# A fused attention and expert kernel: the last pair's half products in another order, one slot later, and the block sums queued ahead of the scalings

## The chip, the cores and the metric

The kernel runs on one core of a Trainium2 chip. The metric is the time of one execution on the device in microseconds; three runs of the kernel before gave 1199.53, 1202.34 and 1204.16 us (median 1202.34). The engines are named as the profile names them: PE is TensorE, which multiplies matrices (PEld is its loading of weights), DVE is VectorE, ACT is ScalarE, POOL is GpSimd and SP is SyncE, which here only issues DMA transfers. Each engine works through its own instructions in the order in which they stand.

## What is computed

There are two stages. The first is an attention without softmax, for 8 batches of 3008 rows; the second is a two-layer network on the 24064 rows that come out.

```python
scores = (1 / S) * z @ z.T                # z: (8, 3008, 64)
attn = maximum(scores, 0) ** 2
x = u * (attn @ v)                        # u, v: (8, 3008, 256)
h = x @ w_in                              # w_in: (256, 2048)
g = h / (1 + exp(-1.702 * h))
out = g @ w_out                           # w_out: (2048, 256)
```

Inputs and output are float32; the kernel multiplies in float16 and accumulates in float32.

## The kernel before, in words

A batch's 3008 rows are cut into six blocks of up to 512. `attend` computes the attention of one block as a list of small steps. The network of a batch follows in 48 calls of `up_group`, which I call slots 0 to 47. One slot makes a 512 x 256 piece of g (a tile `fg` of 256 of the 2048 hidden columns, for one block): four matmuls into `hg` (line 422), gelu by ACT into `gf` (line 435), and a scaling of `gf` into the float16 tile `gt`, by DVE (line 439) or, in slots 17 and up where the slot number modulo 8 is 1, 3 or 5, by ACT (line 437). `hg` shares two PSUM buffers with the score tiles `sc`, and `gf` has two buffers, so the matmuls of slot q wait for the gelu of slot q - 2, and the gelu of slot q for the scaling of slot q - 2.

Slots 0 to 15 are spread over the attention steps of block 4, the others follow the attention of block 5. For all but the end of the last batch, two blocks form a pair (blocks 0 and 1, 2 and 3, 4 and 5), so a pair takes 16 slots: eight tiles, each for both blocks. `TILES` sets the order of the tiles: 0, 4, 1, 5, 2, 6, 3, 7. In even batches block 5 takes part with 384 rows of a pair, and the rest of block 4 is a separate small product (`odd_block`); in odd batches both blocks have 512.

The second layer multiplies a pair as a 2 x 2 arrangement. With a11, a21 the low tiles of the pair's two blocks and a12, a22 the high ones, seven products (P1 to P7) take the place of eight. Four sums of tiles feed them, made by DVE in `pair_sum` for each of four tile pairs m = 0 to 3: S1 = a21 + a22 (line 547), S2 = S1 - a11 (line 549), S3 = a11 - a21 (line 542, written over a21) and S4 = a12 - S2 (line 551). `up_group` appends S1, S2 and S3 of tile pair m to the list `SUMS` in the slot that completes a22, and S4 one slot later; each slot draws one sum from the front of the list, two when it holds over eight.

`pair_product` issues half a product, four of its eight matmuls: the first half with m = 0 and 1, the second with m = 2 and 3 (line 585). P1, P5 and P2 each open a PSUM bank. P6, P7 and P4 go on adding into P1's bank, P3 into P5's. After each product the bank is read: copied into `y` by ACT for P1, P5, P6 and P4 (line 598), or added into `y` by DVE for P3, P7 and P2 (line 600). The next product on a bank can only start when that read has ended.

`products` lists the half products of a batch, and each slot from 16 on takes one from the list behind its `hg` matmuls: slots 16 to 43 run pairs 0 and 1, slots 44 to 47 the first four of the last pair. What is left runs as a tail after slot 47 (10 halves, 11 with the odd block), each step followed by sums still in `SUMS`. `store` turns a finished block on DVE (line 685, into the single buffer `yo`) and writes it by four DMAs from SP; the second block of a pair is stored two slots after its P4. In slots 30 and 36 DVE also turns a block of u for the next batch (line 202). From slot 44 on SP issues transposes for the next batch (line 298), one a slot and one a step of the tail.

The last batch has only two pairs; its blocks 4 and 5 go through `product`, one block at a time with fixed lists of names.

Of the kernel before, what the change touches and what calls it, by code (L numbers as in the profile page):

```python
# [15 lines left out]
def kernel(  # L16
# [24 lines left out]
    NCH = (S + CH - 1) // CH  # L41
# [5 lines left out]
    NFG = NFF // FFG  # L47
# [349 lines left out]
    def blocks(b):  # L397

        return [(i, CH if i < NCH - 1 or b % 2 else LFULL) for i in range(NCH)]

    def paired(b, s):

        return b < B - 1 or s < NCH // 2 - 1

    TILES = (0, 4, 1, 5, 2, 6, 3, 7)

    def up_group(b, q):
        s, r = divmod(q, 2 * NFG)
        pair = paired(b, s)
        if pair:  # L410
            fg, e = TILES[r // 2], r % 2
            if fg >= NFG // 2:
                e = 1 - e
            k = 2 * s + e
        else:
            k, fg = divmod(q, NFG)
        i, n = blocks(b)[k]
        hg = ps2.tile([P, FFG, CH], F32, name="hg", tag="ps2")
        for e in range(FFG):
            ff = fg * FFG + e  # L420
            for c in range(NCC):
                pe.matmul(  # L422
                    hg[:, e, :n], W1[:, c, ff * P:(ff + 1) * P], XT[b, i][:, c, :n],
                    start=(c == 0), stop=(c == NCC - 1),
                )
        if pair:
            if r % 2 == 0:
                GT[b, s, fg, "pair"] = pa.tile([P, FFG, 2, CH], F16, name="gt", tag="tt", bufs=14)
            g = GT[b, s, fg, "pair"][:, :, k % 2, :n]
        else:  # L430
            if fg % 2 == 0:
                GT[b, k, fg // 2] = pa.tile([P, CB, CH], F16, name="gt", tag="tt", bufs=14)
            g = GT[b, k, fg // 2][:, (fg % 2) * FFG:(fg % 2 + 1) * FFG, :n]
        gf = pw.tile([P, FFG, CH], F32, name="gf", tag="gf")
        act.activation(gf[:, :, :n], hg[:, :, :n], AF.Gelu_apprx_sigmoid, scale=1.0 / FSC)  # L435
        if q >= LAGY and q % 8 in (1, 3, 5):
            act.activation(g, gf[:, :, :n], AF.Copy, scale=FSC)  # L437
        else:
            dve.tensor_scalar(g, gf[:, :, :n], FSC, None, ALU.mult)  # L439
        for s_ in [SUMS.pop(0) for _ in range(min(len(SUMS), 1 + (len(SUMS) > 8)))]:  # L440
            s_()
        if pair:
            some = {2: ("S1", "S2", "S3"), 3: ("S4",)}.get(r % 4, ())
            SUMS.extend([lambda m=m, fg=fg: pair_sum(b, s, fg - NFG // 2, m) for m in some])
        elif fg in (NFG - 3, NFG - 1):
            SUMS.extend(left_sums(b, k, fg == NFG - 1))

# [2 lines left out]

    def pairs(b, k):
        return blocks(b)[k][1] // (2 * P)

    SUMS, ST = [], {}
# [32 lines left out]
    def left_sums(b, k, last):  # L490

        some = [("S1", 0), ("S2", 0)]
        if last:
            some = [("S1", 1), ("S2", 1)] + [(name, h) for name in ("S3", "S4") for h in range(2)]
        return [lambda m=m: left_sum(b, k, *m) for m in some]
# [16 lines left out]
    def products(b):  # L512

        lst = []
        for s in range(NCH // 2):
            if not paired(b, s):
                continue
            if s < NCH // 2 - 1:
                order = ["P1", "P1", "P5", "P5", "P6", "P6", "P3", "P3", "P7", "P7", "P2", "P2", "P4", "P4"]
            else:  # L520
                order = ["P1", "P1", "P5", "P2", "P5", "P2", "P6", "P6", "P3", "P3", "P7", "P7", "P4", "P4"]
                if blocks(b)[2 * s + 1][1] < CH:
                    order[6:6] = ["odd"]
            lst += [lambda s=s, m=m, h=order[:x].count(m): pair_product(b, s, m, h) for x, m in enumerate(order)]
        if not paired(b, NCH // 2 - 1):
            k = NCH - 2
            names = [(k, m) for m in ("P1", "P6", "P5", "P7", "P2")] + [(k + 1, "P1"), (k, "P4"), (k, "P3")]
            names += [(k + 1, m) for m in ("P6", "P5", "P7", "P2", "P4", "P3")]
            lst += [lambda k=k, m=m: product(b, k, m) for k, m in names]
        return lst  # L530

    def pair_part(b, s, name):

        f, e = {"a11": (0, 0), "a12": (1, 0), "a21": (0, 1), "a22": (1, 1)}[name]
        w = blocks(b)[2 * s + 1][1]
        return lambda m: GT[b, s, f * NFG // 2 + m, "pair"][:, :, e, :w]

    def pair_sum(b, s, m, name):
        a11, a12, a21, a22 = (pair_part(b, s, x)(m) for x in ("a11", "a12", "a21", "a22"))
        if name == "S3":  # L540
            ST[b, s, name, m] = a21
            dve.tensor_tensor(a21, a11, a21, ALU.subtract)  # L542
            return
        s_ = pa.tile([P, FFG, CH], F16, name="s", tag="a", bufs=26)
        s_ = ST[b, s, name, m] = s_[:, :, :blocks(b)[2 * s + 1][1]]
        if name == "S1":
            dve.tensor_tensor(s_, a21, a22, ALU.add)  # L547
        elif name == "S2":
            dve.tensor_tensor(s_, ST[b, s, "S1", m], a11, ALU.subtract)
        else:  # L550
            dve.tensor_tensor(s_, a12, ST[b, s, "S2", m], ALU.subtract)
# [229 lines left out]
    for b in range(B):  # L781
# [5 lines left out]
        for i in range(NCH):  # L787
# [4 lines left out]
            for n, step in enumerate(attend(b, i, b == 0 and i == 0)):  # L792
                if b == 0 and i == 0 and n in (5, 24):
                    load_u(0, n // 24)
                if b == 0 and i == 0 and n == 2:
                    copies = first_zt(3)
                if b == 0 and i == 0 and n == 3:
                    copies()
                if b == 0 and i == 0 and n in FIRST_CAST:
                    first_cast(FIRST_CAST[n], True)  # L800
                if b == 0 and i == 0 and n in FIRST_ZT:
                    first_zt(FIRST_ZT[n])()
                if (i, n) in turn:
                    turn_u(b, turn[i, n])
                if (i, n) in ((3, 3), (3, 26) if more else (4, 14)) and LAST2:
                    LAST2.pop(0)()
                if (i, n) in load:
                    load_u(b, load[i, n])
                if b == 0 and (i, n) in CASTW:
                    cast_w(CASTW[i, n])  # L810
                if b == 0 and (i, n) in LOADW:
                    load_w(LOADW[i, n])
                if more and (i, n) == (NCH - 2, 2 if b else 16):
                    load_z(b + 1)
                if b == 0 and i == NCH - 1 and n in (8, 30, 42):
                    wsums.pop(0)()
                take(host, sched[i].get(n, 0))
                if i == full(b) and n >= HEAD and (n - HEAD) * LAGY // (2 * NJ - 10) >= head and head < LAGY:
                    up_group(b, head)
                    head += 1  # L820
                step()
        late.sort(key=lambda t: t[0])
        if more:
            for i in range(2):
                load_u(b + 1, i)
            for n0 in range(0, NJ, VB):
                load_v(b + 1, n0)
        prods = products(b)
        for q in range(head, nup):
            if more and q in (head + 14, head + 20):  # L830
                k = int(q == head + 20)
                turn_u(b + 1, k)
                load_u(b + 1, k + 2)
            up_group(b, q)
            if b == 0 and q == head + 3:
                wsums.pop(0)()
            prods.pop(0)()
            for a_ in AFTER:
                a_[0] -= 1
            while AFTER and AFTER[0][0] < 0:  # L840
                AFTER.pop(0)[1]()
            if q >= 44 and late:
                late.pop(0)[1]()
# [42 lines left out]
```

## Time and profile before

| What | Value |
|---|---|
| median of three runs | 1202.34 us (1199.53 to 1204.16) |
| the profiled execution's own time | 1202.51 us |
| its span, first to last instruction | 1200.7 us |
| PE busy | 1171.5 us, 7996 matmuls |
| DVE busy | 862.8 us, 1386 instructions |
| ACT busy | 838.1 us, 941 instructions |
| POOL busy | 214.4 us |
| matmuls of `hg` (line 422) | 354.6 us busy, 1408 |
| gelu on ACT (line 435) | 1003 ns each, 384 |
| scaling on DVE (line 439) | 703 ns each, 288 |
| scaling on ACT (line 437) | 1022 ns each, 96 |
| copies of a bank by ACT (line 598) | 565 ns each, 92 |
| adds of a bank by DVE (line 600) | 665 ns each, 69 |

The span holds eight batches, which look alike in the trace; one is about 148 us long (the tail's matmuls that wait for the sum S1, for instance, lie at 304.51, 451.53 and 600.02 us). [...] A row of the timeline gives the start, the duration, the engine, the line, the operation, what it writes and reads with its shapes, the number of instructions merged, and in brackets the idle time before it with what ended it.

### The profile page before, as it was taken

The page shows a single profiled execution, that of the slowest core. Times are in us where ns is not written, and L with a number is a line of the kernel's source. Part 1 is how long each engine was busy: PE and PEld are TensorE (multiplying, and loading weights), DVE is VectorE, ACT ScalarE, POOL GpSimd, SP SyncE. Part 2 cuts the span into 40 slices and gives each one's busy share as a digit, 9 for nine tenths or more (in the row PEclk, how much of TensorE's full clock was granted, in tenths as well). Part 3 has the DMA queues.
Part 4 walks back from the last instruction along what each step waited for, and adds up shares of the span by engine and source line. Part 5 has one row for each costly group of instructions (what it writes and reads, how often), then busy time and mean ns, then how long its engine had stood idle before and what let it go on. Part 6 is the DMA issues. An engine that isn't in the chain of part 4 may idle for free.

```text
span 1200.7 us, 20853 instructions
## 1 busy us (share of the span) xinstructions
PE 1171.5 (98%) x7996; PEld 576.7 (48%) x7996; DVE 862.8 (72%) x1386; ACT 838.1 (70%) x941; POOL 214.4 (18%) x294
## 2 busy tenths in 40 slices
PE   9999999999999999999999999999999999899998
PEld 3544455444454445544445444554445544455446
DVE  7788866878668775587855877559776597664776
ACT  7878864688646886478864787647876578672785
POOL 3033201231012320133101331014200141101000
PEclk9999999999999999999999999999999999999999
DMA  9999498864898559966499865996559975696023
GB/s 222 210 115 125 86 160 154 96 92 97 152 152 103 89 101 171 147 93 95 95 160 146 103 94 105 167 150 91 92 102 161 141 105 89 108 174 131 1 36 71
DMA packets 459027, 143.47 MB, mean 119 GB/s; under 512 B 424624, under 2 KB 453040, under 8 KB 458928
## 3 DMA queue, kind: packets, MB, share of 16 engines
q1 hardware_dynamic: 402464, 102.36, 52.1%
q0 software_dynamic: 55104, 38.49, 22.0%
q8 instruction: 62, 1.02, 0.4%
q10 hardware_dynamic: 1360, 1.31, 0.3%
q14 instruction: 37, 0.30, 0.1%
HBM read 60.29 MB, written 24.64 MB: 71 GB/s over the span
## 4 chain that ended last, share of the span: by engine, by line
PE 91%; ACT 3%; issue 2%; DVE 2%; DMA 1%; ACTq 0%; POOL 0%; POOLq 0%
PE o L367 38%; PE hg L422 26%; PE st L585 21%; PE sc L235 5%; ACT gf L435 2%; DMA wst<-in_moe_w_in_dram 1%; PE st L631 1%; DVE gt L439 1%; PE yp L559 1%; ACT y L598 0%; DVE y L600 0%; ACT rl L256 0%; DVE s L547 0%; PE w L99 0%; DVE a L270 0%
## 5 line engine op out<-in xcount | busy, mean ns | idle before, releaser
L435 ACT ACTIVATE gf<-hg 128x1024 f32<-128x1024 f32 (+1 forms) x384 | 382.2, 1003 | 124.4 <-PE hg L422 114.2
L256 ACT ACTIVATE rl<-sc 128x1024 f16<-128x1024 f32 (+1 forms) x301 | 287.2, 993 | 141.7 <-PE sc L235 94.7
L422 PE MATMUL hg<-xt,W 128*128 128x512 f16 (+1 forms) x1408 | 354.6, 374 | 1.1 <-ACT gf L435 1.1
L367 PEld LDWEIGHTS <-V 64*128 64x128 f16 (+1 forms) x4098 | 240.4, 94 | 230.6 <-issue 9.3
L367 PE MATMUL o<-a,V 64*128 64x512 f16 (+3 forms) x2278 | 298.2, 368 | 0.3 <-DVE a L270 0.3
L439 DVE TENSOR_SCALAR gt<-gf 128x1024 f16<-128x1024 f32 (+1 forms) x288 | 202.6, 703 | 124.9 <-ACT gf L435 124.5
L270 DVE TENSOR_TENSOR a<-rl 128x1024 f16<-128x1024 f16 (+1 forms) x266 | 178.3, 674 | 126.4 <-ACT rl L256 123.2
L195 POOL DMA_DIRECT2D uq<-in_u_dram x168 | 115.5, 695 | 749.0 <-PE sc L235 550.6
L422 PEld LDWEIGHTS <-W 128*128 128x128 f16 x1536 | 149.6, 98 | 177.2 <-issue 4.2
L367 PE MATMUL o<-tt,V 64*128 64x512 f16 (+1 forms) x1518 | 234.0, 377 | 0.0
L235 PE MATMUL sc<-ZT 64*128 64x512 f16 (+3 forms) x688 | 118.3, 356 | 2.1 <-ACT rl L256 1.5
L585 PEld LDWEIGHTS <-WT 128*128 128x128 f16 x736 | 71.8, 98 | 94.2 <-issue 17.6
L437 ACT ACTIVATE gt<-gf 128x1024 f16<-128x1024 f32 (+1 forms) x96 | 98.1, 1022 | 3.0
L585 PE MATMUL st<-s,WT 128*128 128x512 f16 (+1 forms) x368 | 91.0, 370 | 9.2 <-DVE s L547 9.2
L585 PE MATMUL st<-gt,W 128*128 128x512 f16 (+1 forms) x368 | 92.1, 370 | 5.6 <-DVE gt L439 5.6
L585 PE MATMUL st<-gt,WT 128*128 128x512 f16 (+1 forms) x368 | 88.7, 370 | 4.9 <-DVE y L600 4.9
L598 ACT ACTIVATE y<-st 128x512 f32<-128x512 f32 (+1 forms) x92 | 52.0, 565 | 56.2 <-PE st L585 56.2
L585 PEld LDWEIGHTS <-W 128*128 128x128 f16 x552 | 54.0, 98 | 66.8 <-issue 7.4
L384 DVE TENSOR_TENSOR xt<-o,ut 128x512 f16<-128x512 f32 x80 | 51.4, 685 | 28.5 <-PE o L367 28.5
L600 DVE SCALAR_TENSOR_TENSOR y<-st,y 128x512 f32<-128x512 f32 (+1 forms) x69 | 45.9, 665 | 27.4 <-PE st L585 27.3
L542 DVE TENSOR_TENSOR gt<-gt 128x1024 f16<-128x1024 f16 (+1 forms) x92 | 62.6, 681 | 0.0
L547 DVE TENSOR_TENSOR s<-gt 128x1024 f16<-128x1024 f16 (+1 forms) x92 | 61.9, 673 | 0.0
(65 smaller groups left out, 689.4 us busy)
## 6 DMA issues: line engine op xcount, KB each, us to landing
out_dram<-yo SPq DMA_DIRECT2D x156, 128.0 KB, 2.8
uq<-in_u_dram POOLq DMA_DIRECT2D x140, 128.0 KB, 3.4
V<-in_v_dram POOLq DMA_DIRECT2D x35, 256.0 KB, 6.2
tt<-a SPq DMA_TRANSPOSE x232, 3.4
uq<-in_u_dram POOLq DMA_DIRECT2D x28, 112.0 KB, 4.9
out_dram<-yo SPq DMA_DIRECT2D x28, 96.0 KB, 6.6
uq<-in_u_dram SPq DMA_DIRECT2D x20, 128.0 KB, 4.2
wst<-in_moe_w_in_dram POOLq DMA_DIRECT2D x4, 512.0 KB, 6.2
```

The lines of the kernel that those rows point to most:

```text
L195: eng.dma_start(uq[k * QW:(k + 1) * QW, :n // QW].rearrange("t q c k -> t q (c k)"), src[:, :, cs])
L235: pe.matmul(sc[:, r, :q1 - q0], zt[h, 2 * kp + r, :], zt[h].rearrange("d n p -> d (n p)")[:, q0:q1], start=True, stop=True,)
L256: act.activation(rl[:, :, :n], sc[:, :, :n], AF.Relu, scale=csc)
L270: dve.tensor_tensor(a[:, :, :n], rl[:, :, :n], rl[:, :, :n], ALU.mult)
L367: ins = pe.matmul(acc[c][:, :n], V16[b][h, j].rearrange("p (c k) -> p k c", k=NCC)[:, c], weights(b, i, j)[h], start=(k, m) == first[c], s ...
L422: pe.matmul(hg[:, e, :n], W1[:, c, ff * P:(ff + 1) * P], XT[b, i][:, c, :n], start=(c == 0), stop=(c == NCC - 1),)
L435: act.activation(gf[:, :, :n], hg[:, :, :n], AF.Gelu_apprx_sigmoid, scale=1.0 / FSC)
L437: act.activation(g, gf[:, :, :n], AF.Copy, scale=FSC)
L439: dve.tensor_scalar(g, gf[:, :, :n], FSC, None, ALU.mult)
L542: dve.tensor_tensor(a21, a11, a21, ALU.subtract)
L547: dve.tensor_tensor(s_, a21, a22, ALU.add)
L585: pe.matmul(bank, right[:, ff], lhs[:, f], start=new and ff == 0, stop=ff == NFF // 2 - 1, skip_group_check=True,)
```

## The change

It touches `up_group` and `products`.

In `up_group`, a slot of a pair draws its sums before the scaling and no longer after it, so on DVE they stand ahead of the slot's scaling. New sums are still appended behind the scaling. In slot 46 of a batch, where the last S1, S2 and S3 of the last pair are appended, one more sum is drawn at once. In the first pair of batch 0 the tiles come in the order 0, 1, 4, 5, 2, 6, 3, 7; the order elsewhere stays.

In `products`, an empty entry is put at the front of the list in batches 0 to 6: slot 16 runs no half product, and all half products of these batches come one slot later. Slots 45 to 47 then hold the first three of the last pair, and the tail has 11 halves, 12 with the odd block. The last pair's order is new: first halves of P1, P5 and P2, then the second halves of P1 and P5, all of P6, (the odd block,) the first half of P3, all of P7, the second halves of P3 and P2, and P4. In the last batch, block 4 runs P5 ahead of P6.

```diff
-    TILES = (0, 4, 1, 5, 2, 6, 3, 7)
+    TILES, TILES0 = (0, 4, 1, 5, 2, 6, 3, 7), (0, 1, 4, 5, 2, 6, 3, 7)
...
-            fg, e = TILES[r // 2], r % 2
+            fg, e = (TILES if q >= 2 * NFG or b else TILES0)[r // 2], r % 2
...
         act.activation(gf[:, :, :n], hg[:, :, :n], AF.Gelu_apprx_sigmoid, scale=1.0 / FSC)
+        if pair:
+            some_sums()
         if q >= LAGY and q % 8 in (1, 3, 5):
             act.activation(g, gf[:, :, :n], AF.Copy, scale=FSC)
         else:
             dve.tensor_scalar(g, gf[:, :, :n], FSC, None, ALU.mult)
+        if not pair:
+            some_sums()
+        if pair:
+            some = (("S1", "S2", "S3"), ("S4",))[r % 2] if fg >= NFG // 2 else ()
+            SUMS.extend([lambda m=m, fg=fg: pair_sum(b, s, fg - NFG // 2, m) for m in some])
+            if r == 2 * NFG - 2 and s == NCH // 2 - 1:
+                some_sums()
+        elif fg in (NFG - 3, NFG - 1):
+            SUMS.extend(left_sums(b, k, fg == NFG - 1))
...
+    def some_sums():
         for s_ in [SUMS.pop(0) for _ in range(min(len(SUMS), 1 + (len(SUMS) > 8)))]:
             s_()
-        if pair:
-            some = {2: ("S1", "S2", "S3"), 3: ("S4",)}.get(r % 4, ())
-            SUMS.extend([lambda m=m, fg=fg: pair_sum(b, s, fg - NFG // 2, m) for m in some])
-        elif fg in (NFG - 3, NFG - 1):
-            SUMS.extend(left_sums(b, k, fg == NFG - 1))
...
-                order = ["P1", "P1", "P5", "P2", "P5", "P2", "P6", "P6", "P3", "P3", "P7", "P7", "P4", "P4"]
+                order = ["P1", "P5", "P2", "P1", "P5", "P6", "P6", "P3", "P7", "P7", "P3", "P2", "P4", "P4"]
                 if blocks(b)[2 * s + 1][1] < CH:
-                    order[6:6] = ["odd"]
+                    order[7:7] = ["odd"]
+                lst[:0] = [lambda: None]
...
-            names = [(k, m) for m in ("P1", "P6", "P5", "P7", "P2")] + [(k + 1, "P1"), (k, "P4"), (k, "P3")]
+            names = [(k, m) for m in ("P1", "P5", "P6", "P7", "P2")] + [(k + 1, "P1"), (k, "P4"), (k, "P3")]
```

## The prediction

> **What bounds the kernel now.** I read the page's busy times first, then the waits of TensorE, then the timeline around the places that those waits name.
>
> The page, engines over the whole span:
>
> ```profile
> span 1200.7 us, 20853 instructions
> PE 1171.5 (98%) x7996; PEld 576.7 (48%) x7996; DVE 862.8 (72%) x1386; ACT 838.1 (70%) x941; POOL 214.4 (18%) x294
> PEclk9999999999999999999999999999999999999999
> ```
>
> TensorE (PE) is busy 98% at the full granted clock, and the edit adds or removes no matmul. So all it can win is idle time of PE. What ends that idle time, in the view of waits (who, for whom: us, times, longest):
>
> ```profile
> PE st L585 <- DVE s L547: 9.2, 7, 1.4
> PE st L585 <- DVE gt L439: 5.6, 7, 1.0
> PE st L585 <- DVE y L600: 4.9, 7, 0.8
> ```
>
> Three waits, each once in batches 0 to 6, all in line 585, the half products: 19.7 us together. The timeline places them (start, duration, engine, line, operation, count, idle before). Batch 1, whose last pair is 512 wide in both blocks:
>
> ```profile
> 297.72 0.59 PE L585 MATMUL st<-gt,W 128*128 128x512 f16 x2
> 298.07 0.69 DVE L439 TENSOR_SCALAR gt<-gf 128x1024 f16<-128x1024 f32 x1 [2.00 <-ACT gf L435]
> 298.82 0.59 PE L585 MATMUL st<-gt,W 128*128 128x512 f16 x2 [0.50 <-DVE gt L439]
> ...
> 300.98 1.03 PE L422 MATMUL hg<-xt,W 128*128 128x512 f16 x4
> ...
> 302.70 0.59 PE L585 MATMUL st<-s,WT 128*128 128x512 f16 x2
> 303.16 0.69 DVE L439 TENSOR_SCALAR gt<-gf 128x1024 f16<-128x1024 f32 x1 [0.34 <-ACT gf L435]
> 303.77 0.69 DVE L547 TENSOR_TENSOR s<-gt 128x1024 f16<-128x1024 f16 x1
> 304.51 0.59 PE L585 MATMUL st<-s,WT 128*128 128x512 f16 x2 [1.21 <-DVE s L547]
> ...
> 309.25 1.89 PE L585 MATMUL st<-gt,WT 128*128 128x512 f16 x8
> 311.18 0.69 DVE L600 SCALAR_TENSOR_TENSOR y<-st,y 128x512 f32<-128x512 f32 x1 [0.97 <-PE st L585]
> 311.92 1.89 PE L585 MATMUL st<-gt,WT 128*128 128x512 f16 x8 [0.78 <-DVE y L600]
> ```
>
> First wait: P1's second half, in slot 45, reads a tile whose scaling (slot 44) is just being made. Second: P5's second half reads the last S1, which sits on DVE behind the scaling of slot 47. Third: P4 follows P7 on the same bank, which DVE must first read.
>
> Starts of groups of four, such as hg at 300.98 and the next group at 301.84, lie 0.86 us apart, so a 512 wide matmul takes 0.216 us of PE and a group 0.86 us (0.65 us at 384, by the same reading). Counting from starts, the waits cost 298.82 - 298.15 = 0.67, 304.51 - 303.13 = 1.38 and 311.92 - 310.97 = 0.95 us: 3.0 us a batch. Batches 2, 4 and 6 (and 0) have a last block of 384:
>
> ```profile
> 446.52 0.48 PE L585 MATMUL st<-gt,W 128*128 128x384 f16 x2 [1.03 <-DVE gt L439]
> 451.53 0.49 PE L585 MATMUL st<-s,WT 128*128 128x384 f16 x2 [1.39 <-DVE s L547]
> 459.00 1.46 PE L585 MATMUL st<-gt,WT 128*128 128x384 f16 x8 [0.65 <-DVE y L600]
> ```
>
> By starts (444.99, 449.65 and 456.89 for the groups before them): 1.20 + 1.56 + 0.81 = 3.57 us. In all 3 x 3.0 + 4 x 3.57 = 23.3 us, against 19.7 in the idle column; I go by the starts, since groups without a wait overlap in the rows (1.03 us long, 0.86 apart). [...]
>
> **The change part by part.** For batch 1, let 0 be the moment at which PE ends hg of slot 47.
>
> *One slot later.* An empty entry ahead of the list makes slot 16 run hg alone and moves every product of batches 0 to 6 one slot back; 31 half products instead of 32 lie inside the slots, one more behind them. PE work: zero. What loses cover is hg of slot 17, which now follows hg of slot 16 directly and needs the PSUM pair that the last score tile held. In batch 1 that tile's relu ends at 247.58 and hg of slot 16 streams until 247.64: no wait (batch 2: 396.56 and 396.61). In batch 0 the relu is late:
>
> ```profile
> 100.25 1.02 PE L422 MATMUL hg<-xt,W 128*128 128x512 f16 x4
> 100.59 1.02 ACT L256 ACTIVATE rl<-sc 128x1024 f16<-128x1024 f32 x1 [0.39 <-DVE a L273]
> ```
>
> It ends at 101.61, hg of slot 16 at 101.11: with 0.05 us for the signal (DVE's 311.87 to PE's 311.92), +0.55 us, once. Slots 18 and 19 need gelu of two slots earlier, done 0.5 us or more before.
>
> *P1's second half behind slot 47.* The tile that it reads comes from slot 44 and is done some 3 us earlier: -0.67 (-1.20 at 384). Nothing else is late there: PE has P1, P5, P2 first halves in slots 45 to 47, and their operands are from slot 39 or before. The only bank that one of them waits for is P2's, read by the add of the previous pair's P2, in slot 42.
>
> *Sums ahead of scalings, last S1 drawn in slot 46.* In the built order of batch 1, DVE has: last S4 of tile 2, scaling 46, S1 of tile 3, output transpose, S2, scaling 47, S3, S4. The copy of P4 (0.58) now stands before gelu of slot 45 on ACT, so I let gelu of slot 46 end at -0.06 (hg ends at -1.73, ACT busy until -1.06, 1.0 long). Scaling to 0.68, S1 to 1.36, transpose (1.26) to 2.6, S2 to 3.25, scaling 47 to 3.9, S3 4.6, S4 5.2. PE: P2 half to 0.86, P1 to 1.73, P5 to 2.59, P6 to 4.31, P3 half 5.18, P7 6.90, P3 7.76, P2 8.63, then P4. S1 is needed at 2.16, S2 at 3.88, S3 at 6.5, S4 at 7.3: covered by 0.8, 0.6, 1.9 and 2.1 us. So -1.38 (-1.56 at 384, where S2 keeps 0.2 us).
>
> *Bank reads behind other products.* P4 needs DVE's read of P7: 6.90 + 0.20 + 0.69 + 0.05 = 7.84 against 8.63: covered, -0.95 (-0.81). But P6 now needs ACT's copy of P1 with only P5's half between: 1.73 + 0.19 + 0.60 + 0.05 = 2.57 against 2.59, just covered; at 384: 1.30 + 0.19 + 0.49 + 0.05 = 2.03 against 1.95, +0.08. P7 after P6 has one half of P3 between: again 0 at 512, and behind the odd block at 384. These two have almost no margin; unknown is how late ACT is. From below 0, from above the whole copy, 0.85 us each; I take the lower end, as ACT has nothing queued after gelu of slot 47, which ends at about 1.25.
>
> *Batch 0.* The other tile order (0, 1, 4, 5, ...) starts the sums two slots later, and one sum a slot never catches up: the built order shows the last S1 behind scaling 46, a S3, the output transpose, a S4 and scaling 47. With the rows of 384 (0.56, 0.50, 1.25, 0.50, 0.65, 0.55; gelu 46 ends as slot 47's hg does) it ends at 4.0 after hg of slot 47, and P5 wants it at 0.65 + 0.65 + 0.33 = 1.63: a wait of 2.35 us stands where 1.56 stood. Batch 0 gains 3.57 - 2.35 - 0.55 = 0.7.
>
> *Last batch.* P5 between P1 and P6 takes away the one 0.44 wait there (0.6 by starts), but P7 now follows P6 with only one hg between, and ACT's copy stands behind gelu: about 0.4 back. Gain 0.2; bounds 0 and 0.6.
>
> *DMA queues.* On SP the second output store of a pair moves behind one more transpose (four issues, 2.19 us, beside transposes of about 1.46 us). Eight transposes then end some 7 us into the next batch, whose second tile first reads them some 14 us in: no cost. POOL's order is unchanged.
>
> Sum: batches 1, 3, 5: 3 x 3.0 = 9.0; 2, 4, 6: 3 x (3.57 - 0.08) = 10.5; batch 0: 0.7; last: 0.2. Together 20.4 us. The profiled execution took 1202.51 (span 1200.7 and 1.8 around it), 0.2 from the median of 1202.34: 1202.5 - 20.4 = 1182.1, 1182 for the median too.
>
> [...]
>
> **The rivals.**
>
> *Copies late.* ACT is behind, and P6 and P7 each wait. For it: the margins of 0.02 us. Against: ACT idled 2.01 us before the copy at 305.13. Six batches x 2 x 0.85 = 10.2: 1192.
>
> *The last S1 stays late everywhere, as in batch 0.* Six waits of about 2.3 us where the forecast has none: 20.4 - 6 x 2.3 = 6.6 left: 1195.9. The built order of batches 1 to 6 speaks against it.
>
> *Slower: DVE between slots 28 and 30.* The built order has there, between two scalings, the add into y (0.69), the output transpose (1.25), S3, the input transpose (1.23) and S4 (0.69 each): 4.55 us, plus the scaling 5.2, in two slots of 3.45. Before, add and transpose stood ahead of slot 28's scaling. By my chain the scaling of slot 30 ends at about 274.9 (before: 274.64, with PE 0.86 later), gelu 32 waits 0.3 for its buffer, and hg of slot 34, which needs it, keeps about 1.0 us. Once DVE is over 1.0 us later than that, PE waits; to end above 1208.5 it must cost 26.4 / 7 = 3.8 us in each batch, a backlog that then runs through the following pair. At 4 us each: 1210.
>
> *No change.* The waits only move: 1202. Against: PE's work behind each is longer than what is waited for.
>
> **How the numbers follow.** Forecast 0.77, copies late 0.08, S1 late 0.04, slower 0.07, no change 0.04. A measurement of this kernel tells about 0.5% from no change (6 us): faster 0.88, same 0.05, slower 0.07. The range: from 23.3 + 0.6 of gain, 1178.5, to the copies' rival, 1192; the forecast's own is 1179 to 1186.
>
> **What would show it.** In the waits of the changed kernel, gt, s and y before line 594 (585 now) have shrunk to one s wait of about 2.3 us in batch 0; one hg wait of 0.5 us at about 101; P1's and P6's copies on ACT start within 0.3 us of their product's end. PE's start of a batch's scores moves 3 us up in each batch. Wrong, if waits of st for ACT y, or of hg for gelu, appear in every batch, or the three old ones persist.

## The result, and the profile after

In six runs the changed kernel took 1185.34 us in the median (1180.56 to 1192.90), beside 1202.25 for the kernel before on the same chip: a ratio of 0.9865, 95% interval 0.9831 to 0.9899. The same kernel run again, five times beside eleven runs of the kernel before, gave 1181.94 (1180.72 to 1186.15) against 1201.35, 0.9836 (0.9815 to 0.9858). So it is faster by 16.9 and 19.4 us in the two comparisons, where 20.4 was forecast. The first profiled execution took 1185.92 us (span 1184.1), 16.6 under the profiled one of before.

The page of the changed kernel, engines over the span:

```profile
PE 1171.5 (99%) x7996; PEld 576.6 (49%) x7996; DVE 871.0 (74%) x1386; ACT 837.8 (71%) x941; POOL 214.8 (18%) x294
PEclk9999999999999999999999999999999999999999
```

PE's busy time is 1171.5 as before, and only idle time has gone. The idle stretches of PE above 0.1 us add up to 25.1 us before and 8.4 after. Its waits in the changed kernel (who, for whom: us, times, longest):

```profile
PE hg L422 <- ACT rl L256: 3.0, 2, 2.6
PE st L594 <- DVE s L556: 2.8, 2, 2.1
...
PE hg L422 <- ACT gf L435: 0.5, 2, 0.3
```

The seven waits each for gt and for y are gone. Seven waits for s have become two, both in batch 0, where the prediction had one. Of the two waits of hg for the relu at the top, the longer, 2.6 us, is new and was not foreseen; the other, 0.39 us in slot 17 of batch 0, was. The last pair of batch 1 in the timeline of the changed kernel (start, duration, engine, line, operation, count, idle before), the same stretch as at 302.70 to 311.92 before:

```profile
301.69 1.03 PE L422 MATMUL hg<-xt,W 128*128 128x512 f16 x4
302.42 0.69 DVE L441 TENSOR_SCALAR gt<-gf 128x1024 f16<-128x1024 f32 x1 [1.29 <-ACT gf L435]
302.55 1.89 PE L594 MATMUL st<-gt,W 128*128 128x512 f16 x8
303.15 0.69 DVE L556 TENSOR_TENSOR s<-gt 128x1024 f16<-128x1024 f16 x1
303.75 1.25 DVE L694 STREAM_TRANSPOSE yo<-y 128x1024 f32<-128x1024 f32 x1
304.28 2.75 PE L594 MATMUL st<-s,WT 128*128 128x512 f16 x12
304.48 0.60 ACT L607 ACTIVATE y<-st 128x512 f32<-128x512 f32 x1 [0.64 <-PE st L594]
304.92 0.65 DVE L558 TENSOR_TENSOR s<-s,gt 128x1024 f16<-128x1024 f16 x1
...
309.73 0.69 DVE L609 SCALAR_TENSOR_TENSOR y<-st,y 128x512 f32<-128x512 f32 x1 [2.36 <-PE st L594]
311.19 1.89 PE L594 MATMUL st<-gt,WT 128*128 128x512 f16 x8
...
313.01 0.61 PE L235 MATMUL sc<-ZT 64*128 64x512 f16 x4
```

No PE row here has an idle time. S1 (line 556) ends at 303.84, and the P5 half that reads it starts only at 304.28, behind P2's first and P1's second half; the P1 copy (304.48 to 305.08) ends under that half; and P4, at 311.19, comes after DVE's read of P7 has ended at 310.42, with P3's second half and P2's between. The scores of the next batch start at 313.01 (313.74 before, although the batch had begun 2.16 us sooner there).

The gain by batch, from the moment at which the next batch's scores start (for the last: the end), each against the profiled execution of before:

| Batch | 0 | 1 | 2 | 3 | 4 | 5 | 6 | 7 | sum |
|---|---|---|---|---|---|---|---|---|---|
| forecast | 0.7 | 3.0 | 3.49 | 3.0 | 3.49 | 3.0 | 3.49 | 0.2 | 20.4 |
| first profile | -2.16 | 2.89 | 3.08 | 2.97 | 3.54 | 2.97 | 3.00 | 0.30 | 16.6 |
| second profile (run again) | 3.55 | 2.97 | 3.46 | 2.98 | 3.53 | 2.90 | 3.22 | -0.81 | 21.8 |

Six batches came out within 0.1 us of the forecast or up to 0.5 under it (batches 2 and 6); batch 0 did not, in either profile. The first profile lost time ahead of slot 0. Its timeline there:

```profile
53.79 8.15 SPq L298 DMA_TRANSPOSE tt<-a  x2
...
62.17 1.25 DVE L202 STREAM_TRANSPOSE ut<-uq 128x1024 f32<-128x1024 f32 x1 [4.00 <-DMA uq<-in_u_dram]
...
64.02 0.92 ACT L256 ACTIVATE rl<-sc 128x896 f16<-128x896 f32 x1 [2.68 <-DVE a L270]
...
64.99 1.85 PE L422 MATMUL hg<-xt,W 128*128 128x512 f16 x4 [2.58 <-ACT rl L256]
```

DVE stood 4.00 us before a transpose of u whose load had not landed, ACT's relu waited for DVE, and the first hg for the relu. Two DMA transposes on SP took 8.15 us, where the kernel before spent 4.69 on the same two. The load itself was issued before them: by the trace its four parts went out at 51.49 to 53.19 and landed at 54.94 to 62.15. Then PE ran four matmuls in 1.85 us instead of 1.03. In windows of the same kernel (stretch, length, busy time and instructions of PE, PEld, DVE, ACT and POOL, granted clock, DMA share, GB/s):

```profile
61.60:65.00 3.40, 0.82 (x7) 0.22 (x4) 2.83 (x5) 0.98 (x2) 0.72 (x1) 1.00 1.03 229
65.00:68.40 3.40, 3.40 (x9) 1.21 (x9) 2.59 (x6) 2.63 (x3) 0.00 (x0) 0.51 1.22 208
```

The clock column falls to 0.51 for one window: half speed for 3.4 us costs, by estimate, half of that, some 1.7 us. The page's clock row, 30 us to a digit, does not show it.

### The profile page after: what moved, and what is told of

It is laid out like the page before. It is cut to its first block, busy times and chain, and to the rows that moved or that the text cites. A ratio compares the mean times of both kernels' runs of the same rounds, so it can differ in the third digit from the quotient of the medians.

```text
span 1184.1 us, 20864 instructions
## 1 busy us (share of the span) xinstructions
PE 1171.5 (99%) x7996; PEld 576.6 (49%) x7996; DVE 871.0 (74%) x1386; ACT 837.8 (71%) x941; POOL 214.8 (18%) x294
## 3 DMA queue, kind: packets, MB, share of 16 engines
q10 hardware_dynamic: 1360, 1.31, 0.4%
## 4 chain that ended last, share of the span: by engine, by line
PE 89%; DVE 4%; ACT 2%; DMA 2%; issue 2%; POOL 0%; SPq 0%; DVEq 0%; ACTq 0%; POOLq 0%
PE o L367 37%; PE hg L422 24%; PE st L594 21%; PE sc L235 5%; ACT gf L435 1%; DVE gt L441 1%; PE st L640 1%; DMA uq<-in_u_dram 1%; DMA W<-in_moe_w_out_dram 1%; PE yp L568 1%; ACT rl L256 1%; DVE a L270 0%; DMA zst<-in_z_dram 0%; DVE gt L551 0%; DVE yo L694 0%
## 5 line engine op out<-in xcount | busy, mean ns | idle before, releaser
L558 DVE TENSOR_TENSOR s<-s,gt 128x1024 f16<-128x1024 f16 (+1 forms) x92 | 61.6, 670 | 0.9
```

## The experiments

The theory is the one on record: three waits per batch go, each covered by other products, and batch 0 keeps a late S1 because its tile order lets the sums fall behind. The rivals tested are that the loss at the start belongs to the change, that a part of the edit alone brings the gain, that the empty slot serves only to cover a copy, and that S1 being late would cost little.

**The same kernel again**, to tell whether the start of the first profile belongs to the change.

```diff
(no edit)
```

> The changed kernel once more. Instructions ahead of slot 0 stand in the same order in both kernels, so theory A (the 2.58 us that PE idled at 64.99 us, behind a load of u that landed late, and the half clock of 3.4 us after it, are chance of the start) expects it to be shorter or gone here: the profiled time then is about 1181 to 1183. Theory B (the change causes it) expects the same wait of about 2.6 us and the half clock again. Both expect the waits for S1 in batch 0, 2.1 us at about 157 and 0.7 us at about 133. Median against before: 0.985 to 0.988.

1181.94 us; its profile has neither the wait at the start nor the half clock, and no wait of hg in slot 17 either. The instructions ahead of slot 0 stand in the same order in both kernels, so the late load was chance. (The profile with the other tile order everywhere, further down, has it once more: 1.94 us of idle time at 64.35.) The run also has a chance wait of its own, 0.92 us at 1080.96 for a DMA transpose, in the last batch. What both profiles have are two waits for S1 in batch 0: 0.73 and 2.10 us of idle time in the first, 0.93 and 2.10 here. The second of them, in the timeline of the kernel run again:

```profile
149.41 0.56 DVE L441 TENSOR_SCALAR gt<-gf 128x768 f16<-128x768 f32 x1 [1.01 <-ACT gf L435]
149.88 0.55 DVE L551 TENSOR_TENSOR gt<-gt 128x768 f16<-128x768 f16 x1
150.46 1.25 DVE L694 STREAM_TRANSPOSE yo<-y 128x1024 f32<-128x1024 f32 x1
...
151.63 0.52 DVE L560 TENSOR_TENSOR s<-gt,s 128x768 f16<-128x768 f16 x1
152.07 0.68 DVE L441 TENSOR_SCALAR gt<-gf 128x1024 f16<-128x1024 f32 x1
152.66 0.55 DVE L556 TENSOR_TENSOR s<-gt 128x768 f16<-128x768 f16 x1
153.27 1.79 PE L594 MATMUL st<-s,WT 128*128 128x384 f16 x10 [2.10 <-DVE s L556]
```

This is the order that the prediction read: scaling 46, S3, output transpose, S4, scaling 47, and only then S1.

**The new order of halves alone**, put into the kernel before:

```diff
-                order = ["P1", "P1", "P5", "P2", "P5", "P2", "P6", "P6", "P3", "P3", "P7", "P7", "P4", "P4"]
+                order = ["P1", "P5", "P2", "P1", "P5", "P6", "P6", "P3", "P7", "P7", "P3", "P2", "P4", "P4"]
                 if blocks(b)[2 * s + 1][1] < CH:
-                    order[6:6] = ["odd"]
+                    order[7:7] = ["odd"]
```

> The kernel before with the last pair's new order alone (no slot later, sums as before, the last batch's names as before). The waits for gt (0.67 us at a width of 512, 1.20 at 384, by starts) and for DVE's read of P7 (0.95 and 0.81) go; the wait for the last S1 stays as it was, 1.4 and 1.6 us, since S1 still stands behind the scaling of slot 47 and P1's second half only moves ahead of slot 47's end. P6 does not wait for the copy of P1, as PE waits for S1 in front of it. Gain 3 x 1.62 + 4 x 2.01 = 12.9 us: about 1189.5. If the parts only work together, the gain is under 8 us.

1188.43 us (ratio 0.9893, 0.9873 to 0.9913), 12.9 us under the median of before. In its waits of PE only the one for s is left of the three:

```profile
PE st L585 <- DVE s L547: 9.7, 7, 1.6
```

Batches 1, 3 and 5 gain 1.61 us each (the waits for gt and y, 0.67 + 0.95 = 1.62, were to go), batches 2, 4 and 6 1.70 to 1.82 (2.01 was to go; the wait for S1 grew there from 1.55 to 1.71 us by starts). So two of the three waits are the order's, without the empty slot and without a sum moved. Batch 0 gained 5.24, though its instructions are those of before up to slot 44: some 3 us of that is chance in the start of the profiled execution of before, which has two single waits, 1.13 us at 73.42 and 1.15 at 97.04, that this kernel's profile lacks. The first of the two follows a load of weights that ACT waited 1.29 us for, at 71.41. Gains of batch 0 against that execution are read with this in mind.

**The sums alone**, in front of the scalings and with the extra draw in slot 46; the halves in their old order, no empty slot, the old tile order. Against the changed kernel:

```diff
-            fg, e = (TILES if q >= 2 * NFG or b else TILES0)[r // 2], r % 2
+            fg, e = TILES[r // 2], r % 2
...
-                order = ["P1", "P5", "P2", "P1", "P5", "P6", "P6", "P3", "P7", "P7", "P3", "P2", "P4", "P4"]
+                order = ["P1", "P1", "P5", "P2", "P5", "P2", "P6", "P6", "P3", "P3", "P7", "P7", "P4", "P4"]
                 if blocks(b)[2 * s + 1][1] < CH:
-                    order[7:7] = ["odd"]
-                lst[:0] = [lambda: None]
+                    order[6:6] = ["odd"]
...
-            names = [(k, m) for m in ("P1", "P5", "P6", "P7", "P2")] + [(k + 1, "P1"), (k, "P4"), (k, "P3")]
+            names = [(k, m) for m in ("P1", "P6", "P5", "P7", "P2")] + [(k + 1, "P1"), (k, "P4"), (k, "P3")]
```

> The kernel before with the sums alone moved: drawn ahead of the scaling, one more drawn in slot 46 of the last pair; tile order, product order, slots and the last batch's names as before. The wait for the last S1 goes in all seven batches (1.38 us at 512, 1.56 at 384): gain 3 x 1.38 + 4 x 1.56 = 10.4 us, about 1192. The waits for gt and for DVE's read of P7 stay, 0.5 and 1.0 us, 0.8 and 0.65 us in the idle column. With order_only (12.9) the parts add up to the 23.3 us of the three waits. Rival: drawing sums ahead of scalings delays scalings and gelu, and hg waits for ACT in many slots; then the gain is under 5 us.

1192.19 us (0.9921, 0.9903 to 0.9939). The wait for s is gone; in the waits of PE the one for y stands as before, and the one for gt comes 14 times instead of 7:

```profile
PE st L593 <- DVE gt L441: 7.4, 14, 1.0
PE st L593 <- DVE y L608: 4.9, 7, 0.8
```

The timeline of the same kernel, batch 2, shows what the second seven are:

```profile
444.42 0.56 DVE L555 TENSOR_TENSOR s<-gt 128x768 f16<-128x768 f16 x1
445.01 0.56 DVE L557 TENSOR_TENSOR s<-s,gt 128x768 f16<-128x768 f16 x1
445.49 0.69 DVE L441 TENSOR_SCALAR gt<-gf 128x1024 f16<-128x1024 f32 x1
...
446.23 0.48 PE L593 MATMUL st<-gt,W 128*128 128x384 f16 x2 [0.28 <-DVE gt L441]
```

P2's second half reads the tile of slot 47, whose scaling now stands behind S1 and S2 on DVE. The new order puts that half last but two, and so covers it. The expected 1192 came out although these seven waits were not in it, so that agreement is partly luck: in batches 1 to 6 the profiles differ by 6.1 us, where 8.8 was expected. That is why the parts do not add up to the whole: 1.61 + 1.05 = 2.66 in a batch with two blocks of 512, where both together gain 2.97.

**Without the empty slot**, all else as in the changed kernel:

```diff
-                lst[:0] = [lambda: None]
```

> The changed kernel without the empty entry: no slot later, all else kept. My account: the three waits stay away, but P1's second half now ends in slot 47 and its copy stands on ACT behind gelu of slot 47, so P6 waits for it, 0.2 us at 512 and 0.5 us at 384 in each of batches 1 to 6, 2.1 us together; batch 0 gets back the 0.4 us of hg in slot 17. About 1 to 2 us slower than the changed kernel, 1183 to 1187. If the slot later is what takes the old waits away, some 1195.

1187.23 us (0.9879, 0.9858 to 0.9900). P6 was to wait for P1's copy; no such wait stands in the profile, so what the expectation named as the cost was wrong, though the time came out near it. Batches 1, 3 and 5 still gain 2.81 to 2.88, and batches 2, 4 and 6 only 1.84 to 2.57, for a wait on S1. Timeline of this kernel, batch 2:

```profile
446.53 1.25 DVE L693 STREAM_TRANSPOSE yo<-y 128x1024 f32<-128x1024 f32 x1 [0.15 <-DMA out_dram<-yo]
...
448.15 0.53 DVE L441 TENSOR_SCALAR gt<-gf 128x768 f16<-128x768 f32 x1
448.72 0.56 DVE L555 TENSOR_TENSOR s<-gt 128x768 f16<-128x768 f16 x1
...
449.33 0.97 PE L593 MATMUL st<-s,WT 128*128 128x384 f16 x5 [0.80 <-DVE s L555]
```

Without the empty slot P4 of the middle pair comes one slot sooner, so its store does too: the output transpose now stands ahead of S4, scaling 46 and S1 on DVE, and P5 waits for S1. In batch 0, where the sums are late anyway, the waits for S1 are 1.80 and 2.27 us.

**Without the empty slot, but with that store held one slot longer**, to tell whether the place of the transpose is all that the empty slot gives:

```diff
-                lst[:0] = [lambda: None]
...
-            AFTER.append([2, lambda: store(b, 2 * s + 1)])
+            AFTER.append([3 if s else 2, lambda: store(b, 2 * s + 1)])
```

> The changed kernel without the empty entry, and with the output transpose of pair 1's second block one slot later, which puts it behind the last S1 on DVE again. In the run without the empty entry P5 waited for S1 in the batches of 384 (0.74 to 1.15 us, idle column), and not P6 for P1's copy as I had expected. If the transpose ahead of S4, scaling 46 and S1 is the cause, that wait goes and the time is about 1183, close to the changed kernel: what the slot later is worth is this order on DVE. If the missing cover on PE (a quarter of P5 fewer behind slot 47) is the cause, it stays at about 1187.

1185.39 us (0.9873, 0.9854 to 0.9892), between the two expectations. Batches 2, 4 and 6 gain 2.73 on average, where the kernel without the empty slot gained 2.17 and the changed kernel, run again, 3.40. So of the 1.23 us that the empty slot brings there, 0.56 are the transpose's place, and the rest is cover: by starts, S1 is still waited for 0.33 us and S2 0.21 (P1's copy, 0.09, is waited for in the changed kernel too). These are means of three batches in single profiles, which spread by up to 0.7 us; with the first profile of the changed kernel (3.21) the 1.23 would be 1.04. In batch 0 the two waits for S1 are 1.80 and 2.71 us here, 1.5 us more than in the changed kernel run again, and with the 0.67 that is missing in each of the three batches this comes to the 3.5 us by which the two medians differ.

**The old tile order in batch 0 as well:**

```diff
-            fg, e = (TILES if q >= 2 * NFG or b else TILES0)[r // 2], r % 2
+            fg, e = TILES[r // 2], r % 2
```

> The changed kernel with the old tile order 0, 4, 1, 5, ... in the first pair of batch 0 too, all else kept. If the two waits for S1 in batch 0 (0.9 us in pair 1, 2.1 us in the last pair, idle column) come from sums that start two slots later under the other tile order and never catch up, both go: 3.3 us less by starts, about 1178.5 against 1181.9 of the changed kernel. If they come from the missing half product in slot 16 or from the start of the batch, they stay. No half clock after the first microseconds.

1178.31 us (1177.16 to 1179.76, four runs, against 1201.17; ratio 0.9812, 0.9797 to 0.9826): the fastest of all, 22.9 us under the kernel before. All its waits of PE:

```profile
PE w L99 <- DVE nil L75: 1.2, 1, 1.2
PE sc L235 <- ACT ZT L143: 0.4, 1, 0.4
PE zp L135 <- DVE zst L128: 0.2, 1, 0.2
PE hg L422 <- ACT gf L435: 0.2, 1, 0.2
```

Both waits for S1 are gone, and the first three lines belong to the start. The granted clock of its four runs is 1.000, that of the eleven runs of the changed kernel 0.993 to 1.000. The tile order of batch 0 is the part of the change that costs.

**Another cure for batch 0**: its tile order kept, two sums drawn as soon as more than three are queued.

```diff
-            some_sums()
+            some_sums(3 if b == 0 else 8)
...
-    def some_sums():
-        for s_ in [SUMS.pop(0) for _ in range(min(len(SUMS), 1 + (len(SUMS) > 8)))]:
+    def some_sums(most=8):
+        for s_ in [SUMS.pop(0) for _ in range(min(len(SUMS), 1 + (len(SUMS) > most)))]:
```

> The changed kernel with its new tile order, but in batch 0 a slot draws two sums when more than three are waiting (in the changed kernel: more than eight). The tile order itself then is not undone, only the arrears. Same expectation as for the old tile order: both waits for S1 in batch 0 gone, about 1178.5. If the tile order does harm by itself, the waits stay in part.

1179.84 us (0.9830, 0.9811 to 0.9849). The waits for S1 are gone here too, so the backlog of sums was their cause, whichever way it is cleared. But with two sums ahead of a scaling something else is late. Timeline of this kernel, batch 0:

```profile
79.25 1.02 ACT L435 ACTIVATE gf<-hg 128x1024 f32<-128x1024 f32 x1 [1.45 <-DVE gt L441]
80.33 1.02 PE L422 MATMUL hg<-xt,W 128*128 128x512 f16 x4 [0.34 <-ACT gf L435]
...
85.06 1.02 PE L422 MATMUL hg<-xt,W 128*128 128x512 f16 x4 [0.47 <-ACT gf L435]
```

Gelu waits 1.45 us for the scaling that frees its buffer, and hg for the gelu. The chain is that of the slower rival (DVE late, gelu late, hg late), in another place and at 0.3 to 0.5 us. A third wait of hg for gelu, 0.65 us at 72.92, is of another kind: ACT had waited 0.81 us for a load of weights at 70.90.

**The other tile order in the first pair of every batch**, to price the rival "S1 late everywhere":

```diff
-            fg, e = (TILES if q >= 2 * NFG or b else TILES0)[r // 2], r % 2
+            fg, e = (TILES if q >= 2 * NFG else TILES0)[r // 2], r % 2
```

> The changed kernel with the other tile order 0, 1, 4, 5, ... in the first pair of every batch but the last, so that the sums are two slots in arrears in all of batches 0 to 6. My account of the rival in the prediction: in each of batches 1 to 6 a wait for S1 of about 0.9 us in pair 1 and of 2.1 to 2.5 us in the last pair appears, 6 x 3.3 = 20 us: about 1202, no faster than the kernel before. If waits of over 2.2 us bring the half clock (3.4 us at half speed after 2.27 and 2.58 us of idle in two runs, none after 2.10), up to 10 us more. If arrears matter in batch 0 alone, 1182.

1212.01 us (1206.28 to 1216.36; ratio 1.0089, 1.0060 to 1.0117): slower than the kernel before, by the upper of the expected cases. The edit reaches the first pair of the last batch too, which the expectation left out. Waits of PE, and two windows of the same kernel that each follow the last S1 wait of a batch (batch 2, then batch 1; columns as above):

```profile
PE st L594 <- DVE s L556: 22.4, 15, 2.5
```

```profile
457.40:460.80 3.40, 3.40 (x19) 2.05 (x17) 1.16 (x3) 0.98 (x2) 0.00 (x0) 0.51 1.00 165
310.70:314.10 3.40, 3.40 (x18) 1.56 (x16) 1.30 (x3) 1.19 (x2) 0.00 (x0) 1.00 1.02 181
```

After the wait in batch 2 the clock is 0.51, after the one in batch 1 it stays 1.00. In the profiled execution (1216.36) there are fifteen waits for S1 (two in each of batches 0 to 6, one in the last), 22.4 us of idle time or 24.8 with the 0.16 by which the idle column reads each one short, and six windows at half clock (granted clock 0.992 over the span), by estimate 10.2 us. Added to the 1177.16 of the kernel with the old tile order they make 1212.1; waits of hg and of scores for the relu, 2.3 + 1.6 us in this profile, bring it to about 1216. The sum is rough: it leaves out two short waits for S2 and S4 in the last batch, 0.9 us together. The prediction had priced this rival at six waits in the last pairs; it left out those of the middle pairs, the last batch and the half clock.

## Why the prediction was right, and where it was not

**Right, with its mechanism.** PE's idle time was the only thing to win, and three waits were it. By the order alone the gt and y waits go at 1.61 us a batch (1.62 forecast), by the sums the one for S1. In batch 1 of the changed kernel, counted from the end of hg of slot 47 (302.55), S1 ended at 1.29 (1.36 forecast), S2 at 3.02 (3.25), scaling 47 at 3.63 (3.9), S3 at 4.23 (4.6) and S4 at 4.83 (5.2), and P4 began at 8.64 (8.63).

**The nearly empty margins held.** P1's copy ended at 2.53, with the signal (0.05) at 2.58 beside the 2.59 at which P6 wanted it: P6 follows without a gap. In the blocks of 384, P6 started 0.09 us late at 442.68 of the second profile (0.08 forecast), and the same at 731.76 and 1021.16. The rival "copies late" did not happen.

**Batch 0: right in kind, one wait missed.** The last S1 was late by 2.26 us by starts (2.35 forecast). But the term counted the backlog only at the last pair. In the middle pair S1 waited as well, 0.73 and 0.93 us of idle time, 0.9 and 1.1 by starts, behind another output transpose. The wait of hg in slot 17 came in one profile (0.39 idle, 0.55 forecast) and not in the other, where the relu was not late.

**The start was not in the sum at all.** The table's -2.16 in the first profile comes together thus: +3.57 for the old waits, -2.26 and -0.9 for S1, -0.55 for hg, -2.7 - 1.7 for the late load with its half clock, +2.6 for the two single waits of the profiled execution of before; that makes -1.9. The chance of one start is as large as a batch's gain, so single profiles of 16.6 and 21.8 and medians of 16.9 and 19.4 all belong to one kernel. The forecast of 20.4 less the missed wait of 1.0 is 19.4; that one of the two medians meets this figure exactly is luck, as the other is 2.5 us away. The slowest of the six first runs, 1192.90 us, has a granted clock of 0.993 over its span, the other five 0.998 or 0.999; it has no trace, so where it lost its time is open.

**The price of a sum ahead of a scaling.** The sums-alone run prices it: sums in front of scalings everywhere, and 9.2 us faster. The first profile has a case where it does cost, in slot 15 of batch 2 (timeline):

```profile
377.93 1.23 DVE L202 STREAM_TRANSPOSE ut<-uq 128x1024 f32<-128x1024 f32 x1
...
379.10 0.64 DVE L556 TENSOR_TENSOR s<-gt 128x1024 f16<-128x1024 f16 x1
...
379.67 0.67 DVE L441 TENSOR_SCALAR gt<-gf 128x1024 f16<-128x1024 f32 x1
...
380.44 1.02 ACT L435 ACTIVATE gf<-hg 128x1024 f32<-128x1024 f32 x1 [1.31 <-DVE gt L441]
...
381.51 1.02 PE L422 MATMUL hg<-xt,W 128*128 128x512 f16 x4 [0.23 <-ACT gf L435]
```

A transpose of u and then S1 stand ahead of the scaling, gelu waits 1.31 us, hg 0.23. The same comes in batch 6 (0.31 at 960.14), and these are the two batches in which the first profile gained about 3.0 where its batch 4 gained 3.54. That this chain is the whole difference is not shown: the second profile has no such wait of 0.1 us or more, and its batch 6 gained only 3.22. The slower rival's chain is thus real, but the price that would decide it, 3.8 us a batch, is far off, and slot 34, where it was sought, shows nothing. By these rows the sum put ahead holds the scaling back by 0.57 us (379.10 to 379.67). In the last pair of batch 1, where DVE had been idle for 1.29 us before the scaling at 302.42, S1 and S2 stand ahead of scaling 47 too (303.15, 304.92 and 305.49), and there they cost PE nothing: no PE row has an idle time.

**The last batch** gained 0.3 in most profiles of kernels with its new list (0.2 forecast). It gained nothing in the two kernels that keep the old list (-0.01, -0.02), so P5 ahead of P6 does it. The exceptions are the kernel run again and the other tile order everywhere, whose waits there are named above, and the kernel with the store held longer (-0.06), which waits another 0.13 us of idle time there, for a sum at 1174.99.

**What the empty slot is for** was read wrongly behind the prediction: in the expectation for the kernel without it, it was cover for a copy. About half of its worth in the batches of 384 lies in DVE's queue, where it moves a store's transpose behind S1; the other half is cover, for S1 and S2.

Open is what makes the load at the start late. The slow DMA transposes go with it: of the ten profiles, five have the two transposes at 7.43 to 8.15 us, and in these DVE waits 0.69 to 4.00 us for the load; in the other five they took 4.65 to 4.87 us, and DVE does not wait. Two of the slow five are kernels with neither the empty slot nor the other tile order, so the change does not bring it, and only in two did PE stop at the first hg (2.58 and 1.94 us). What slows both is not shown.

## What to carry to other kernels

When PE is busy 98%, list its waits, find what stands ahead of each late operand on the engine that makes it, and move consumers behind independent products that are longer than the lateness; then price the edit's parts alone, since an order that removes one wait can cover the one that another part creates. The backlog of sums on DVE was carried along until something drained it: the other tile order, two slots at the front of batch 0, was paid in its middle and last pair (0.93 and 2.10 us of idle time of PE in the kernel run again), and these waits are gone where two sums were drawn as soon as more than three were queued. An edit that delays or advances one queue entry also moves the stores and transposes that hang on it, so read every engine's built order, not only that of the engine one means to help.

## What was not expected of the hardware

A wait of PE cost more than its length where a stretch at half clock came after it. In the kernel without the empty slot, a wait of 2.27 us in batch 0, ending at 157.11, was followed by 3.4 us at half clock, by the estimate above another 1.7 us (columns as above):

```profile
154.00:157.40 3.40, 1.13 (x8) 0.58 (x6) 3.37 (x8) 1.37 (x2) 0.00 (x0) 0.99 0.68 118
157.40:160.80 3.40, 3.40 (x18) 1.97 (x16) 1.18 (x3) 0.98 (x2) 0.00 (x0) 0.50 1.04 178
```

In the first profile of the changed kernel the clock is 0.50 from 65.04 to 68.45 us, after the wait of 2.58, and 1.00 in the 3.4 us on either side. With the other tile order everywhere, 2.08 us of idle time in batch 2 (452.00 to 457.10) were enough. The two S1 waits of 2.10 us in the profiles of the changed kernel were not followed by a half clock: in the first, PE was busy for 1.38 of the 3.40 us from 155.50 to 158.90, and the clock stays 1.00 to 164.80; in the second, for 1.33 of the 3.40 us from 151.20 to 154.60, and it is 1.00 there and to 158.00. Nor was the one of 2.71 us in the kernel with the store held longer, whose clock is 1.000 over the span, where one such stretch makes 0.999 of it in the first profile. So the length of a wait alone, 2.2 us in the expectation for the other tile order everywhere, does not tell which ones are followed by a half clock. What does is not shown.

The other surprise is the spread of the DMA at the start: the same two transposes took 4.69 and 8.15 us, and a load of u landed late enough to stop DVE for 4.00 us in one execution and not at all in the next of the same kernel.
